# Values in whole rows with edge columns, ones written over them by GpSimd, and a new order table, in a chain of attention, a gated MLP and a gMLP

## The chip, the cores and the metric

The kernel runs on one core of a Trainium2 chip. That core has engines that work side by side, each through its own queue: TensorE (PE: matmuls, and PEld for its weight loads), VectorE (DVE), ScalarE (ACT), GpSimd (POOL) and SyncE (SP), which here issues nearly all DMAs. The metric is the device time of one execution in microseconds (us), as a median of several runs.

## The reference

Three layers run one after the other, on 2 batches of 768 positions. The attention has 8 heads of 64 and sees, for each position, the first 8 positions and the 96 last ones, with a slope per head as bias:

```python
keep = is_global | is_local
dist = np.where(is_global & ~is_local, float(n_local), np.abs(rel).astype(np.float32))
scores = scale * np.matmul(q, k.transpose(0, 1, 3, 2)) + -slopes[:, None, None] * dist
scores = np.where(keep, scores, -1000000000.0)
a = np.exp(scores - np.max(scores, axis=-1, keepdims=True))
a = a / (np.sum(a, axis=-1, keepdims=True) + 1e-09)
x = np.matmul(a, v)
```

Its output, as 768 x 512 per batch, goes into an MLP of width 1024 whose hidden layer is gated by a convolution over positions, and then into a gMLP with a 768 x 768 product over positions:

```python
h = np.maximum(x @ w_in, 0.0)                       # 512 -> 1024
gate = 1.0 / (1.0 + np.exp(-conv_out))              # conv_out: 3 taps over positions of h
x = h * gate @ w_out                                # 1024 -> 512
h = np.maximum(x @ w_in, 0.0)                       # gMLP, 512 -> 1024
u, v = h[..., :512], h[..., 512:]
v_s = np.einsum('ts,bsd->btd', w_spatial, normalized(v)) + b_spatial[None, :, None]
out = (u * v_s) @ w_out                             # 512 -> 512
```

All is fp32. The matmuls of the two MLPs use fp16 pairs, a high half and a low half of each operand (names that end in h and l).

## The kernel before

**Tiling.** A group g is one batch and one of three chunks of 256 positions, so there are six groups. Each group has four head pairs; a pair with its group is a unit u. For a unit the kernel computes score products (line 789, fp32, from a tile `qk`), a reduction with bias and mask and the row's minimum (DVE, line 808), the exponential (ACT, line 826), a transposition of the result on PE (line 839) and the product with the values (line 894), which is divided by its row sum (lines 906 to 911) and transposed again (line 942) into one 128x256 piece of x. PE's high copy of x is written by ACT (456) or DVE (460), the low one by DVE (line 470). Four pieces make the x of a group. Then come eight matmul tasks `inner` of the first MLP (line 1017, twelve matmuls each), which need all four pieces, their convolution and gate, and the outer matmuls (line 1087). The gMLP follows (lines 1171, 1294, 1382, 1444). Weights arrive as packed 128x512 `raw` tiles, are decoded on POOL (659), ACT (655) and DVE (665, 670) and split into high and low halves.

**The values.** Groups 0 and 1 (`PLAINS`) use their values in fp32; the other four split them into halves. The product at line 894 takes 65 columns a head: 64 values and a column of ones, which gives the row sum. The pair's tile therefore has 130 columns (`VW`): a one, 64 values, 64 values, a one. There is a single tile `v_dt_float_89` for both groups. `v_load` (line 726) writes the ones once, by a POOL memset ahead of group 0's load, and loads 128 values at a time between the edge columns, 512 B for each of 12 or 16 pieces of a partition. Group 1's load writes the same inner columns again and leaves the ones.

**The order.** Each piece of work is a task with a list of the tasks it depends on. A table, `ORDER`, lists all tasks: two signs for the task's number, one for its engine (P, D, A, G for POOL, S for SP), and for a task that opens a PSUM bank the number of that bank. `Plan.emit` issues the tasks in that order, so the table fixes the sequence in every engine's queue, including the choice of engine where two could do it; semaphores then only make an instruction wait, they don't change the sequence. `emit` also puts fill-in matmuls on constant data (line 988, 128x256) in front of those PE tasks that the planner expects to wait in the first 70 planned us, in a number that it works out from the planned gap; they are in the program for good.

**DMAs.** SP issues its loads in table order at line 514; a load whose tile is still in use makes SP wait, with all later loads behind it.

## Time and profile before

| | |
|---|---|
| time, median of 3 runs | 346.76 us (346.62 to 347.51) |
| the profiled execution's own time | 346.18 us |
| its span, first to last instruction | 344.4 us |
| mean granted TensorE clock | 0.996 |
| PE busy | 336.9 us (98%) |
| DVE busy | 305.3 us (89%) |
| ACT busy | 244.0 us (71%) |
| POOL busy | 140.6 us (41%) |

The span is cut into stretches in the rows below: how long each engine was busy in a stretch, then the granted clock (1.00 is 2.4 GHz), the mean busy share of the 16 DMA engines and the rate at which they moved bytes. A timeline's row is one run of like instructions with its start and its duration; the bracket, where there is one, gives the idle time just before it and what ended it. Matmuls overlap in PE's pipeline, so the distance between two starts is the time that a matmul costs, and its own duration is longer.

### The profile page before, as it was taken

What the parts mean: (1) busy time and instruction counts of PE and PEld (TensorE: products, weight loads), DVE (VectorE), ACT (ScalarE), POOL (GpSimd) and SP (SyncE); (2) the same over time, 40 slices, a digit from 0 to 9 for tenths busy, and PEclk for the clock granted to TensorE, in tenths of its full rate; (3) what the DMA queues carried; (4) which work ended last, traced back from release to release, by engine and by line L of the source; (5) the groups of instructions that cost most, each with busy time, mean ns of one, the idle gap of its engine ahead of it and who ended that gap; (6) DMA issues with size and microseconds to landing.
All of it is one profiled execution on the core that took longest, in us unless ns stands there. A gap on an engine that the chain in (4) does not pass through costs nothing.

```text
span 344.4 us, 7937 instructions
## 1 busy us (share of the span) xinstructions
PE 336.9 (98%) x2824; PEld 246.5 (72%) x2824; DVE 305.3 (89%) x892; ACT 244.0 (71%) x619; POOL 140.6 (41%) x233
## 2 busy tenths in 40 slices
PE   8999999999999999999999999999999999999993
PEld 5888779898888888888996757755556666654451
DVE  6999999999999999999988899999998999999400
ACT  4999999999999999999865552776555233334331
POOL 5747698599757877737451000000124012010000
PEclk9999999999999999999999999999999999999998
DMA  7999638799659984645770000001461000000332
GB/s 246 349 386 300 214 105 302 175 209 256 125 149 205 278 173 79 184 79 109 102 221 0 2 1 0 2 1 48 126 206 52 0 2 0 3 30 0 124 124 101
DMA packets 46115, 43.62 MB, mean 127 GB/s; under 512 B 34674, under 2 KB 36466, under 8 KB 45554
## 3 DMA queue, kind: packets, MB, share of 16 engines
q1 hardware_dynamic: 46064, 43.02, 45.7%
q8 instruction: 24, 0.39, 0.5%
q14 instruction: 25, 0.20, 0.2%
q10 hardware_dynamic: 2, 0.00, 0.0%
HBM read 31.48 MB, written 3.15 MB: 101 GB/s over the span
## 4 chain that ended last, share of the span: by engine, by line
PE 96%; DMA 1%; DVE 0%; ACT 0%; issue 0%; DVEq 0%
PE bank L1017 19%; PE bank L1087 18%; PE bank L1294 12%; PE bank L1444 9%; PE bank L1382 9%; PE bank L1171 9%; PE bank L789 7%; PE bank L894 4%; PE bank L839 2%; PE bank L988 2%; PE bank L942 2%; DMA qk_dt_float<-in_qk 1%; PE bank L900 1%; PE bank L901 1%; PE bank L902 1%; ACT wk_dt_float L454 0%
## 5 line engine op out<-in xcount | busy, mean ns | idle before, releaser
L1017 PE MATMUL bank<-x_dt_float,w1h_dt_float 128*128 128x260 f16 (+1 forms) x384 | 65.5, 273 | 0.0
L1087 PE MATMUL bank<-hh_dt_float,w2h_dt_float 128*128 128x256 f16 (+2 forms) x192 | 52.4, 273 | 0.0
L1017 PE MATMUL bank<-x_dt_float,w1l_dt_float 128*128 128x260 f16 (+1 forms) x192 | 52.4, 273 | 0.0
L1087 PE MATMUL bank<-hl_dt_float,w2h_dt_float 128*128 128x256 f16 (+2 forms) x192 | 52.3, 272 | 0.0
L1087 PE MATMUL bank<-hh_dt_float,w2l_dt_float 128*128 128x256 f16 (+2 forms) x192 | 52.3, 272 | 0.0
L1030 DVE SCALAR_TENSOR_TENSOR bank<-hp_dt_float,cwt,bank 128x254 f32<-128x254 f32 (+2 forms) x96 | 46.1, 486 | 3.3 <-ACT bank L1024 0.6
L470 POOL TENSOR_TENSOR ph_dt_float<-sb_dt_float,ph_dt_float 128x512 f16<-128x512 f32 x29 | 34.2, 1184 | 20.5 <-ACT ph_dt_float L456 12.4
L1017 PEld LDWEIGHTS <-w1h_dt_float 128*128 128x128 f16 x384 | 37.1, 97 | 5.7
L1087 PEld LDWEIGHTS <-w2h_dt_float 128*128 128x128 f16 x384 | 36.3, 98 | 5.4 <-issue 0.3
L808 DVE CUSTOM_DVE_ANT_0 sb_dt_float<-bank,bias_dt_float 128x256 f32<-128x256 f32 (+1 forms) x96 | 35.4, 402 | 1.6 <-PE bank L789 1.3
L1382 PE MATMUL bank<-ys_dt_float,w3uh_dt_float 128*128 128x384 f16 x128 | 31.2, 326 | 0.0
L826 ACT ACTIVATE sb_dt_float<-sb_dt_float,nb_dt_float 128x256 f32<-128x256 f32 (+1 forms) x64 | 29.6, 491 | 0.0
L659 POOL TENSOR_SCALAR raw_dt_float<-raw_dt_float 128x512 int32<-128x512 uint8 x28 | 19.0, 680 | 24.7 <-DMA raw_dt_float<-in_w 22.0
L1444 PE MATMUL bank<-w4h_dt_float,g_dt_float 128*128 128x512 f16 (+1 forms) x104 | 28.8, 363 | 0.0
L1171 PE MATMUL bank<-w3vh_dt_float,ys_dt_float 128*128 128x512 f16 x96 | 28.5, 379 | 0.0
L470 POOL TENSOR_TENSOR hl_dt_float<-ac_dt_float,hh_dt_float 128x254 f16<-128x254 f32 (+2 forms) x35 | 23.4, 678 | 10.7 <-DVE hh_dt_float L460 8.0
L1444 PEld LDWEIGHTS <-g_dt_float 128*128 128x128 f16 x156 | 15.2, 98 | 15.4
L1171 PEld LDWEIGHTS <-ys_dt_float 128*128 128x128 f16 x144 | 14.1, 98 | 15.3
L1294 PE MATMUL bank<-ws_dt_float,vn_dt_float 128*128 128x384 f16 x144 | 25.0, 326 | 0.0
L1050 ACT ACTIVATE bank<-bank 128x254 f32<-128x254 f32 (+2 forms) x48 | 16.9, 364 | 10.5 <-DVE bank L1030 10.2
L1024 ACT ACTIVATE bank<-hp_dt_float,cwt 128x254 f32<-128x254 f32 (+2 forms) x44 | 21.0, 477 | 0.5
L1055 DVE SCALAR_TENSOR_TENSOR ac_dt_float<-bank,hp_dt_float 128x254 f32<-128x254 f32 (+2 forms) x48 | 19.5, 418 | 2.0 <-ACT bank L1050 1.5
(198 smaller groups left out, 907.6 us busy)
## 6 DMA issues: line engine op xcount, KB each, us to landing
raw_dt_float<-in_w SPq DMA_DIRECT2D x20, 512.0 KB, 6.3
qk_dt_float<-in_qk SPq DMA_DIRECT2D x24, 336.0 KB, 4.6
v_dt_float<-in_vb SPq DMA_DIRECT2D x4, 1024.0 KB, 5.7
out_x<-wk_dt_float SPq DMA_DIRECT2D x11, 256.0 KB, 2.0
raw_dt_float<-in_wst SPq DMA_DIRECT2D x6, 384.0 KB, 3.8
raw_dt_float<-in_w3v SPq DMA_DIRECT2D x4, 512.0 KB, 5.5
raw_dt_float<-in_w3u SPq DMA_DIRECT2D x4, 512.0 KB, 4.4
v_dt_float<-in_vb SPq DMA_DIRECT2D x2, 768.0 KB, 5.1
```

The source lines that it names most:

```text
L470: self.engines[e].tensor_tensor(out=out, in0=in0, in1=in1, op=ALU.subtract)
L789: nc.tensor.matmul(self.ps(sp[h])[:, 256 * t : 256 * (t + 1)], x[r, t * P : (t + 1) * P], y[r, k0[t] : k0[t] + 256], start=n == 0, stop=n ...
L808: nc.vector.tensor_tensor_reduce(out=sb[:, h, :n], in0=self.ps(self.sp[u][h])[:, 256 * t : 256 * t + n], in1=self.m("bias", 2 * p + h)[:, ...
L826: nc.scalar.activation(out=sb[:, h, :n], in_=sb[:, h, :n], func=AF.Exp, scale=-1.0, bias=nb[:, h : h + 1])
L1017: nc.tensor.matmul(self.ps(acc)[:, :nx], w[f][:, k * P : (k + 1) * P], x[:, k, x0:], start=k == n == 0, stop=k == 3 and n == 2,)
L1024: nc.scalar.activation(out=ac(), in_=near(1), func=AF.Copy, scale=tap(1))
L1030: nc.vector.scalar_tensor_tensor(out=ac(), in0=near(j), scalar=tap(j), in1=ac(), op0=ALU.mult, op1=ALU.add)
L1087: nc.tensor.matmul(ps(), w[2 * d + k // 4][:, k % 4 * P : (k % 4 + 1) * P], x, start=k == n == 0, stop=k == 7 and n == 2,)
L1171: nc.tensor.matmul(ps(), x[:, y, k, tk], w[k], start=n == 0, stop=n == 11)
L1294: self.nc.tensor.matmul(self.ps(acc)[:, :HS], v[:, k, x, ek], w[:, k, y], start=n == 0, stop=n == 8)
L1382: nc.tensor.matmul(ps(), w[e4][:, k * P : (k + 1) * P], x[:, y, k, s], start=n == 0, stop=n == 11)
L1444: nc.tensor.matmul(ps(), x[:, y, k, tk], w[k][:, at], start=n == 0, stop=n == 11)
```

## The change

The host now packs a second array of values, `vp`, for groups 0 and 1: the layout of the tile with its edge columns, filled with copies of the neighbouring values. `v_load` loads whole rows of it, 1560 or 2080 floats a partition, 6,240 or 8,320 B in one piece. The load covers the edge columns too, so the memset of the ones is now a task behind each load, two in all. The whole order table is replaced. Lines from 735 of the kernel before on carry numbers that are three lower in the kernel after.

```diff
 ORDER = (
-    "CHSAAGAWSDnGAnSAXGABDACGAZSADDAuSAbGAgSAEDBHGCMDAFPAGDCJA0CIGAHDAaP12AJDAKAASAAIDAMAAoGAdDBaSApA3AyDAYSANGAcDAOA",
...
+    "AAGAWSCISEIGAuSAbGABDBIGDoGAnSADDAZSD2GACGAgSAEDCNDAFPAaP12CKA0AGDCJGFLGAHDAJDAQAASAAIDBiP34BbSAKAA0DAoGAMAAdDAX",
...
 class Kernel:
-    def __init__(self, ctx, tc, vb, qk, qf, kf, vf, nw, w1, cw, w2, w3u, w3v, wst, bsp, w4, out):
+    def __init__(self, ctx, tc, vb, vp, qk, qf, kf, vf, nw, w1, cw, w2, w3u, w3v, wst, bsp, w4, out):
...
         if g in PLAINS:
-            v = self.m("v").rearrange("p (n d) -> p n d", d=VW)
-            if g == 0:
-                self.ones_beside(v, ("v", g, "one"))
-            self.load(
-                v[:, : n * NPAIR, 1 : 1 + 2 * D], self.vb[b, c, :, :n].rearrange("p a (n d) -> p (a n) d", d=2 * D),
-                [("v", g, "v")], n * P * 2048, [("v", g, "one")],
-            )
+            size = n * NPAIR * VW
+            v = self.m("v")[:, :size]
+            self.load(v, self.vp[g, :, :size], [("v", g)], 4 * P * size)
+            self.ones_beside(v.rearrange("p (n d) -> p n d", d=VW), ("v", g, "one"))
             return
...
     vb = np.stack(rows, axis=1).reshape(B, NCH, 4, P, DM).transpose(0, 1, 3, 2, 4)
+    vp = vb.reshape(B * NCH, P, 4, NPAIR, 2 * D)[: len(PLAINS)]
+    vp = np.concatenate([vp[..., :1], vp, vp[..., -1:]], axis=-1).reshape(len(PLAINS), P, -1)
```

The new table moves instructions on every engine. Three places follow; the names are tiles, and the number behind a name is its buffer. First DVE, before the kernel's first matmul of line 1017. `x_dt_float_156` is the low half of x for group 0, and its row is the last of the four pieces. This is the queue of the kernel before:

```order
L911 TENSOR_TENSOR xk_dt_float_159<-bank,r_dt_float_161 128x256
L670 SCALAR_TENSOR_TENSOR wk_dt_float_138<-raw_dt_float_137,bank 128x512
L665 SCALAR_TENSOR_TENSOR bank<-bank,raw_dt_float_126 128x512
L470 TENSOR_TENSOR x_dt_float_156<-bank,x_dt_float_155 128x256
L808 ISA sb_dt_float_132,nm_dt_float_147<-bank,bias_dt_float_82 128x256
L808 ISA nm_dt_float_147 128x1
L670 SCALAR_TENSOR_TENSOR wk_dt_float_136<-raw_dt_float_126,bank 128x512
```

And this is the same place after:

```order
L908 TENSOR_TENSOR xk_dt_float_159<-bank,r_dt_float_161 128x256
L665 SCALAR_TENSOR_TENSOR bank<-bank,raw_dt_float_126 128x512
L805 ISA sb_dt_float_139,nm_dt_float_153<-bank,bias_dt_float_82 128x256
L805 ISA nm_dt_float_153 128x1
L805 ISA sb_dt_float_139,nm_dt_float_153<-bank,bias_dt_float_83 128x256
L805 ISA nm_dt_float_153 128x1
L470 TENSOR_TENSOR x_dt_float_156<-bank,x_dt_float_155 128x256
L670 SCALAR_TENSOR_TENSOR wk_dt_float_136<-raw_dt_float_126,bank 128x512
```

Two reductions of a later unit (line 805, with the short row that reads out their minimum) stand ahead of the piece of x instead of one behind it; a decoding step (line 670) has left the place.

The second place is SP's queue, where the loads of about 33 to 50 us stand; the two `raw` loads of `in_w` are those that the trace shows from 38.60 us on. Before:

```order
L514 DMA qk_dt_float_122<-in_qk 128x672
L514 DMA raw_dt_float_128<-in_w 128x512
L514 DMA raw_dt_float_137<-in_w 128x512
L514 DMA qk_dt_float_88<-in_qk 128x672 x2
L514 DMA qk_dt_float_130<-in_qk 128x672
L514 DMA raw_dt_float_142<-in_w3v 128x512
```

After:

```order
L514 DMA qk_dt_float_122<-in_qk 128x672
L514 DMA raw_dt_float_128<-in_w 128x512
L514 DMA qk_dt_float_88<-in_qk 128x672
L514 DMA qk_dt_float_130<-in_qk 128x672
L514 DMA raw_dt_float_137<-in_w 128x512
L514 DMA qk_dt_float_122<-in_qk 128x672
L514 DMA qk_dt_float_88<-in_qk 128x672
L514 DMA v_dt_float_89<-in_vb 128x2048
```

Two `qk` loads have moved ahead of the second `raw` load.

The third place is POOL's queue around the second memset of the ones, which the kernel before doesn't have; there the single memset stands at the queue's beginning. After:

```order
L659 TENSOR_SCALAR raw_dt_float_126<-raw_dt_float_126 128x512
L1036 MEMSET hp_dt_float_178 128x1
L659 TENSOR_SCALAR raw_dt_float_137<-raw_dt_float_137 128x512
L659 TENSOR_SCALAR raw_dt_float_142<-raw_dt_float_142 128x512
L729 MEMSET v_dt_float_89 128x16x2
L470 TENSOR_TENSOR w1l_dt_float_103<-wk_dt_float_129,w1h_dt_float_95 128x512
```

The memset (line 729) stands behind three decodes of `raw` tiles (line 659). On SP, the loads of two of these three, `raw_dt_float_126` and `raw_dt_float_142`, are issued behind the load of `v`. The first memset of the kernel after stands on POOL behind two decodes and six mask sums (line 607).

## Rows read from the trace of the kernel before

**Rows 1.** The page: busy time, share, instructions; shares of the last chain.

```profile
PE 336.9 (98%) x2824; PEld 246.5 (72%) x2824; DVE 305.3 (89%) x892; ACT 244.0 (71%) x619; POOL 140.6 (41%) x233
...
PE 96%; DMA 1%; DVE 0%; ACT 0%; issue 0%; DVEq 0%
```

**Rows 2.** By stretch: us, busy PE, PEld, DVE, ACT, POOL, clock, DMA, GB/s.

```profile
0.00:70.00 70.00, 68.20 (x550) 55.68 (x551) 64.78 (x222) 64.06 (x157) 47.55 (x85) 1.00 0.77 259
70.00:340.00 270.00, 268.71 (x2277) 190.80 (x2274) 240.51 (x671) 179.97 (x463) 93.03 (x149) 1.00 0.39 93
...
10.00:20.00 10.00, 10.00 (x84) 8.51 (x83) 9.25 (x38) 9.89 (x23) 7.98 (x12) 1.00 1.05 378
20.00:30.00 10.00, 9.88 (x86) 8.50 (x85) 9.24 (x29) 9.58 (x23) 4.99 (x6) 1.00 0.89 315
```

**Rows 3.** Timeline of the end: start, us, engine, line, operation.

```profile
338.33 0.38 PE L1444 MATMUL bank<-w4l_dt_float,g_dt_float 128*128 128x512 f16 x1
```

**Rows 4.** Line 988 alone: count, ns min/median/max, first and last start.

```profile
L988 PE MATMUL bank<-hl_dt_float x60: 272/273/421, 1.2 to 53.0; 128*128 128x256 f16 x60
```

**Rows 5.** Timeline of PE from 39 to 56 us.

```profile
42.00 1.04 PE L988 MATMUL bank<-hl_dt_float 128*128 128x256 f16 x8
...
48.94 0.93 PE L988 MATMUL bank<-hl_dt_float 128*128 128x256 f16 x7
50.10 1.14 PE L789 MATMUL bank<-qk_dt_float 64*128 64x256 f32 x8 [0.23 <-DMA qk_dt_float<-in_qk]
```

**Rows 6.** Timeline of PE around the first matmul of line 1017.

```profile
28.03 0.38 PE L1017 MATMUL bank<-x_dt_float,w1h_dt_float 128*128 128x256 f16 x2
...
29.34 0.38 PE L1017 MATMUL bank<-x_dt_float,w1h_dt_float 128*128 128x256 f16 x2
```

**Rows 7.** Timeline of DVE around the last piece of group 0's x.

```profile
27.06 0.41 DVE L470 TENSOR_TENSOR x_dt_float<-bank,x_dt_float 128x256 f16<-128x256 f32 x1
27.39 0.41 DVE L808 CUSTOM_DVE_ANT_0 sb_dt_float<-bank,bias_dt_float 128x256 f32<-128x256 f32 x1
27.73 0.08 DVE L808 DVE_READ_ACCUMULATOR2_ANT nm_dt_float<- 128x1 f32 x1
```

**Rows 8.** Timeline of SP's queue: start of the issue, us, what is loaded.

```profile
7.98 0.39 SPq L514 DMA_DIRECT2D v_dt_float<-in_vb  x1
...
25.11 0.68 SPq L514 DMA_DIRECT2D v_dt_float<-in_vb  x1
...
28.48 4.52 SPq L514 DMA_DIRECT2D raw_dt_float<-in_w  x4
...
38.60 6.49 SPq L514 DMA_DIRECT2D raw_dt_float<-in_w  x2
```

**Rows 9.** By stretch, as rows 2, where the v loads and others move.

```profile
10.00:12.50 2.50, 2.50 (x22) 1.87 (x22) 2.23 (x11) 2.49 (x7) 2.26 (x4) 1.00 1.06 301
...
21.00:24.00 3.00, 2.88 (x27) 2.59 (x26) 2.67 (x13) 2.83 (x7) 0.02 (x1) 1.00 1.03 412
27.00:30.00 3.00, 3.00 (x29) 2.58 (x28) 2.79 (x8) 2.93 (x7) 2.13 (x3) 1.00 0.88 272
```

**Rows 10.** Timeline of PE at the first product with v.

```profile
13.22 0.66 PE L839 MATMUL bank<-ident,sb_dt_float 128*128 128x128 f32 x4
13.71 0.56 PE L894 MATMUL bank<-v_dt_float,pt_dt_float 128*128 128x65 f32 x4
```

**Rows 11.** Timeline of POOL, at its start and before 14 us.

```profile
1.40 0.14 POOL L732 MEMSET v_dt_float<- 128x32 f32 x1
...
12.87 0.99 POOL L607 TENSOR_TENSOR bias_dt_float<-bias_dt_float,keep_dt_float 128x288 f32<-128x288 f32 x1 [0.45 <-DVE nm_dt_float L808]
```

**Rows 12.** The page: POOL's decodes; raw loads, last number median us to landing.

```profile
L659 POOL TENSOR_SCALAR raw_dt_float<-raw_dt_float 128x512 int32<-128x512 uint8 x28 | 19.0, 680 | 24.7 <-DMA raw_dt_float<-in_w 22.0
...
raw_dt_float<-in_w SPq DMA_DIRECT2D x20, 512.0 KB, 6.3
```

**Rows 13.** Waits before 60 us: us in total, times, longest.

```profile
POOL raw_dt_float L659 <- DMA raw_dt_float<-in_w: 9.3, 3, 4.5
```

More of the change, by code (lines that the diff above doesn't have):

```diff
@@ L170 @@
+    "DcoDcLDcpP4cnDcXDcYGcxP1crDcRGctDcvDb4GdiP5dQDdRDc0P0dSDb-Db_DcAAauDdrP7cEDa7DcGAcFDa8DcqDc9Dc3DdDP4c4Dc-DdoP2dE",
+    "DcdDc_DceGdADdBDdJP6dpAcyDdsAdqScMAdtSdcP2dKDcSAdWDcZAdjDduP7cfAczDc1DdXDdkDdlDd3P1dFDddDdTDdGDdeDdfDdxP0c5Dd4Ad",
+    "HDd5Sc6GdLDdgDdmDd0P5dMDdyAdvDclAdNDdwSc7AdYDdzSdCAdZDdaDd_P4dIAdOAdUAdbAeLP2dhAeADdnAd1AeCP1d2SeBSd6P6d8P7d7DeM",
+    "AeDAeNSeOP0d9Ad-SeESeIP3eFP4ePAeJAeQSeKSeGAeHS",
 )
@@ L1692, in pack @@
     arrays = dict(
-        vb=vb, qk=qk, qf=qt, kf=kt, vf=vfull,
+        vb=vb, vp=vp, qk=qk, qf=qt, kf=kt, vf=vfull,
         nw=np.stack([np.asarray(n_global), np.asarray(n_local)]).astype(np.int64).view(np.uint16),
```

106 lines of the change are left out of this document (51 added, 55 removed).

## The prediction

> **What bounds the kernel now.** I read the page from the top and then went to the trace. TensorE (PE) is busy 336.9 us of the 344.4 us span, and the chain that ended last is 96% PE [rows 1]. A busy PE need not be a useful one, so the next view is the one by stretch [rows 2]: from 70 to 340 us PE is busy 268.71 us, and its last matmul begins at 338.33 [rows 3], so next to nothing is idle in between. The first 70 us are different. There PE lacks 1.80 us, and part of what counts as busy is no work at all: 60 fill-in matmuls on constant data (line 988), all between 1.2 and 53.0 us [rows 4]. In the same stretch, from 10 us on, DVE and ACT are busy 9.2 to 10 us of every 10 [rows 2]. So the kernel has two parts: an opening in which DVE and ACT feed PE and the gaps are filled with line 988, and 270 us in which PE alone sets the pace. What the opening loses is not given back, because PE has no gap later in which to catch up. The change can therefore move the end by what it does to PE in the opening, and by what it does to the last few us.
>
> **The fill-in matmuls.** They stand in PE's queue and run whether needed or not, so their number is a cost of the program itself. Eight of them take 1.04 us [rows 5], of which the last one's own 0.27 [rows 4]: (1.04 - 0.27) / 7 = 0.11 us each. Counted in the two orders, the program before has 60 and the program after 66. Fifteen stand before the first score products in both. Before the first matmul of line 1017 there are 30 before and 38 after: +8 x 0.11 = +0.88. Behind it, 30 before and 28 after: -2 x 0.11 = -0.22. Together +0.66 us.
>
> **The DVE piece behind those eight.** The first matmul of line 1017 (28.03) [rows 6] needs the last of four 128x256 pieces of x, which DVE began to write at 27.06 [rows 7]. In the new order four more line-808 reductions of 256 columns stand ahead of that piece (two of them are in the fences on DVE). One takes 27.39 to 27.73, 0.34 us, to the next instruction's start [rows 7], so 4 x 0.34 = 1.36 us more DVE work. DVE has little room there, 9.24 us of the 10 from 20 to 30 us are busy [rows 2], so little of the 1.36 can be hidden. The eight fills already occupy 0.88 of it. What is left is between 0 (hidden) and 0.48 us; I take 0.25, the middle.
>
> **The queue of SP at 45 us.** PE ran seven fills from 48.94 and started the score products only at 50.10, named as released by the DMA of a qk load [rows 5]: 1.16 us, of which 7 x 0.11 = 0.77 were fills and 0.39 bare waiting. That load stood behind two raw loads that waited for their buffers, 6.49 us from 38.60 [rows 8]; the new order puts it and the next qk load ahead of the second of them (the fences on SP). The fills are counted already. The bare 0.39 us may go, between 0 and 0.39; I take 0.2 as gained.
>
> **The loads themselves.** The first v load is issued at 7.98 [rows 8] and its 512-byte pieces (12 for each of 128 partitions) flow at 301 GB/s in the stretch behind, with the DMA engines at 1.06, where raw and qk loads reach 412 GB/s at 1.03 [rows 9]. Moved at 412, its 128 x 6,240 B = 0.80 MB take 1.94 us in place of 0.79 MB / 301 = 2.61 us: 0.7 us of DMA time saved. For the second, 1.05 MB at the 272 GB/s of its stretch [rows 9] is 3.86 us, and 1.065 MB at 412 would be 2.58: 1.3 saved. None of it lies on the path: PE entered the first product with v at 13.71 with no idle named there, straight behind a transposition at 13.22 [rows 10]. What the freed DMA time gives to the raw and qk loads behind it is the rival below. If the loads stay slow, this term stays nil as well.
>
> The Trainium skill, "DMA: Bandwidth & Descriptors", section "Specifications", puts the least transfer for line rate at 512 B, and these pieces are exactly 512 B. By that the whole-row form saves nothing, the loads keep their length and only the memset's lateness would grow. The trace disagrees, 301 against 412 GB/s, so the measurement decides.
>
> **The memsets of the ones.** One memset before (0.14 us at 1.40) [rows 11], two after. They stand on POOL, which is busy 140.6 of 344.4 us [rows 1], so their own time costs at most 0.3 us there and nothing on PE. The new thing is the wait: POOL now waits for the v load to land, with its decodes and low halves of the weights queued behind it, and PE's v products wait for POOL. The first has two decodes and six mask sums (line 607) ahead of it in the new order; before, POOL began the last of these sums at 12.87 and it took 0.99 [rows 11], so POOL comes to the memset near 12 to 14 us, about when the load is in; bounds 0 to 0.5 us. I take 0, since four more fills (0.44 us) stand on PE ahead of the first product with v, 27 against 23. The second memset is a rival.
>
> **The end.** The last two PE tasks, their ACT copies and the last output load are the same in both orders. From the start of the last matmul (338.33) [rows 3] to the end of the span at 344.4 nothing changes: 0, within +-0.2.
>
> **Sum.** +0.66 + 0.25 - 0.2 + 0 = +0.7 us (between +0.3 and +1.2). The profiled execution took 346.18 us, 0.58 below the median of the three runs, 346.76. Profiled, the new kernel would take 346.9; against the median 347.5.
>
> **Rivals.**
> *The second memset is late (slower).* In the new POOL order the memset over group 1's v stands behind three raw decodes, two of whose loads are issued behind that v load. Before, PE's product with it needed the load alone. PE gets to it in the new order at about 28.03 + 0.88 (first line-1017 product), five products of 1.31 (28.03 to 29.34) [rows 6], one score product of 1.14 [rows 5], two transpositions of 0.49 (13.22 to 13.71) [rows 10] and a fill: 37.7 us. The v load of before went out at 25.11 and the raw loads behind it from 28.48 over 4.52 us, so the last near 32.6 [rows 8]; a raw load lands in 6.3 us (median), 38.9, one decode is 0.68 (19.0 us / 28) [rows 12], memset by 39.6: 1.9 us late. With the v load 1.3 us shorter the price is 0.6. It decides from the point where that memset ends after 37.7. For it: POOL waited 9.3 us for raw loads in the first 60 us, the longest 4.5 [rows 13]. Against: the raw load that went out at 28.48 need not be as late if buffers free sooner. Time: 347.5 + 0.6 to 1.9, so about 349.
>
> *The gaps close (faster).* The bare waits of PE around the fills shrink: 0.39 at 50.10 [rows 5], and a part of the 1.80 us that PE lacks in the first 70 [rows 2], most of it in the first 10. An estimate from the two for what can close is 1.1 us, while the fills stay at +0.66: -0.4 us, 346.3. And where DMA is full, above 1.0 from 10 to 20 us [rows 2], the 0.7 us saved on the first v load may bring everything behind it forward by as much, decodes and x pieces included: -1.1, 345.7. Against it: DVE has more to do before the first line-1017 product, and the fills are there to be run in any case.
>
> *The change does not do what it says.* The rows are split again by the DMA engines, 272 GB/s stays: only the memset rival grows, to 349.4.
>
> **How the numbers follow.** A measurement of this kernel can tell about 0.3% (1.04 us) from no change. Forecast case (+0.3 to +1.2, a seventh of it beyond 1.04): 0.58. Late memset or another new wait in the opening (+1.0 to +2.9): 0.24. Closing gaps (-1.6 to +0.2): 0.18, six tenths of it beyond 0.3%. So faster 0.11, slower 0.08 + 0.23 = 0.31, within 0.58. The range takes in the forecast with both bounds, the closing gaps down to -1.1 and the late memset to its upper part: 345.7 to 349.1.
>
> **What the new profile would show.** The first matmul of line 1014 (1017 before) at 28.9 to 29.4. Line 985 (988 before) 66 times. The score product that started at 50.10 no longer ends a wait for DMA. A stretch from 70 us on with PE idle nowhere. More than 400 GB/s while the first v load moves, and no PE wait named after POOL's memset of v. I am wrong if the first product of group 1 waits for that memset, if PE shows idle time after 70 us, or if the opening ends no later than before although it holds six more fills.

## The result, and the profile after

The kernel after takes 349.44 us (median of 10 runs, 348.11 to 352.22), the kernel before took 347.08 in the same session (10 runs, 346.39 to 347.51). The ratio is 1.0075, with an interval of [1.0047, 1.0102]: slower, by 2.4 us where +0.7 was forecast, and above the range's end of 349.1. The profiled execution took 348.64 us, its span is 346.6, its mean granted clock 0.999.

The page of after, against [rows 1] (busy time, share, instructions; shares of the last chain):

```profile
PE 337.3 (97%) x2830; PEld 246.9 (71%) x2830; DVE 302.4 (87%) x874; ACT 244.9 (71%) x625; POOL 155.1 (45%) x246
...
PE 82%; DVE 6%; DMA 5%; issue 2%; POOL 2%; ACT 1%; SPq 0%; DVEq 0%; ACTq 0%; POOLq 0%
```

PE works only 0.4 us more. The chain that ended last was 96% PE before; now 14% of it runs through DVE, DMA, POOL and ACT: PE is waiting for others in places where it didn't. By stretch, with the columns of [rows 2]:

```profile
0.00:70.00 70.00, 66.69 (x545) 54.91 (x546) 64.69 (x222) 63.08 (x153) 47.43 (x85) 1.00 0.76 250
70.00:340.00 270.00, 269.50 (x2284) 191.68 (x2282) 237.75 (x655) 181.26 (x472) 107.66 (x162) 1.00 0.38 95
```

In the first 70 us PE lacks 3.31 us where it lacked 1.80: 1.51 more, and 6 fills (0.66) come on top. Behind it 0.50 us are idle. The tail is as long as before; its start is 2.36 us later than in [rows 3]:

```profile
340.69 0.38 PE L1441 MATMUL bank<-w4l_dt_float,g_dt_float 128*128 128x512 f16 x1
```

The view of waits says which of PE's waits are named in the first 100 us (total, times, longest). Of after:

```profile
PE bank L985 <- DVE hl_dt_float L538: 1.2, 1, 1.2
PE bank L891 <- POOL v_dt_float L729: 1.0, 2, 0.5
PE bank L786 <- DMA qk_dt_float<-in_qk: 0.9, 2, 0.7
PE bank L1014 <- DVE xk_dt_float L908: 0.3, 1, 0.3
```

The first row is the start of the program and stands in before too. The other three are new or grown: before, PE never waited for the memset or for line 908's tile, and only 0.23 us for a qk load [rows 5]. In PE's timeline (start, us, operation, and in the bracket the idle time just ahead of it and its releaser) the five waits are these:

```profile
8.54 1.13 PE L786 MATMUL bank<-qk_dt_float 64*128 64x256 f32 x8 [0.69 <-DMA qk_dt_float<-in_qk]
...
14.02 2.00 PE L891 MATMUL bank<-v_dt_float,pt_dt_float 128*128 128x65 f32 x16 [0.47 <-POOL v_dt_float L729]
...
37.98 2.00 PE L891 MATMUL bank<-v_dt_float,pt_dt_float 128*128 128x65 f32 x16 [0.51 <-POOL v_dt_float L729]
...
40.17 1.13 PE L786 MATMUL bank<-qk_dt_float 64*128 64x256 f32 x8 [0.20 <-DMA qk_dt_float<-in_qk]
...
80.44 0.38 PE L1014 MATMUL bank<-x_dt_float,w1h_dt_float 128*128 128x260 f16 x2 [0.34 <-DVE xk_dt_float L908]
```

They add up to 2.21 us, close to the 2.36 by which the end moved. That such a list is not yet a cause is what the experiments had to show: taking away two of these waits changed nothing.

### The profile page after: what moved, and what is told of

Read it like the earlier page. It is cut to its first block, busy times and chain, and to the rows that moved or that the text cites. A ratio compares the mean times of both kernels' runs of the same rounds, so it can differ in the third digit from the quotient of the medians.

```text
span 346.6 us, 7949 instructions
## 1 busy us (share of the span) xinstructions
PE 337.3 (97%) x2830; PEld 246.9 (71%) x2830; DVE 302.4 (87%) x874; ACT 244.9 (71%) x625; POOL 155.1 (45%) x246
## 2 busy tenths in 40 slices
DMA packets 44707, 43.65 MB, mean 126 GB/s; under 512 B 34674, under 2 KB 34930, under 8 KB 44146
## 4 chain that ended last, share of the span: by engine, by line
PE 82%; DVE 6%; DMA 5%; issue 2%; POOL 2%; ACT 1%; SPq 0%; DVEq 0%; ACTq 0%; POOLq 0%
PE bank L1084 17%; PE bank L1014 14%; PE bank L1291 12%; PE bank L1441 9%; PE bank L1379 9%; PE bank L1168 9%; PE bank L786 4%; DMA pt_dt_float<-ph_dt_float 2%; PE bank L891 2%; DMA qk_dt_float<-in_qk 2%; DVE bank L665 2%; PE bank L939 2%; POOL bias_dt_float L607 1%; PE bank L897 1%; PE bank L899 1%
## 5 line engine op out<-in xcount | busy, mean ns | idle before, releaser
L1084 PE MATMUL bank<-hh_dt_float,w2h_dt_float 128*128 128x254 f16 (+2 forms) x192 | 52.3, 273 | 0.1
L1084 PE MATMUL bank<-hh_dt_float,w2l_dt_float 128*128 128x254 f16 (+2 forms) x192 | 52.3, 273 | 0.0
L1084 PE MATMUL bank<-hl_dt_float,w2h_dt_float 128*128 128x254 f16 (+2 forms) x192 | 52.3, 273 | 0.0
L470 POOL TENSOR_TENSOR hl_dt_float<-ac_dt_float,hh_dt_float 128x254 f16<-128x254 f32 (+2 forms) x37 | 25.0, 684 | 16.9 <-ACT hh_dt_float L456 13.2
L1441 PEld LDWEIGHTS <-g_dt_float 128*128 128x128 f16 x156 | 15.2, 98 | 15.4
L1358 ACT ACTIVATE hp_dt_float<-bank 128x260 f32<-128x260 f32 (+1 forms) x44 | 16.7, 382 | 6.6 <-DVE ac_dt_float L1052 3.3
L454 ACT ACTIVATE wk_dt_float<-bank 128x512 f32<-128x512 f32 (+1 forms) x11 | 5.8, 555 | 21.6 <-PE bank L1441 15.6
```

The source lines that it names most:

```text
L470: self.engines[e].tensor_tensor(out=out, in0=in0, in1=in1, op=ALU.subtract)
L1084: nc.tensor.matmul(ps(), w[2 * d + k // 4][:, k % 4 * P : (k % 4 + 1) * P], x, start=k == n == 0, stop=k == 7 and n == 2,)
L1441: nc.tensor.matmul(ps(), x[:, y, k, tk], w[k][:, at], start=n == 0, stop=n == 11)
```

## Experiments: the loads, the memsets and the table apart

In all of these, the fills stand in fixed places and number (those of the table that the kernel uses), so that an edit doesn't move them.

**e1_load_only.** The new loads and both memsets under the old table; the second memset's task was put on POOL behind the low half of w2's first block (at 33.70 us in its trace). The head of the loop over a load's pieces and the old memset, which go as well, are left out of the cut ("...").

```diff
...
-            self.load(
-                v[:, : n * NPAIR, 1 : 1 + 2 * D], self.vb[b, c, :, :n].rearrange("p a (n d) -> p (a n) d", d=2 * D),
+            self.load(v, self.vp[g, :, :size], [("v", g)], 4 * P * size)
+            self.ones_beside(v.rearrange("p (n d) -> p n d", d=VW), ("v", g, "one"))
```

> The new load alone: the kernel before, with its own order and its 60 fill-in matmuls at their places, but values of groups 0 and 1 in whole rows and two memsets of the ones behind them. The first memset stands on POOL where the changed kernel has it, behind the six mask sums; the second stands right behind the low half of w2's first block, near 32.5 us. Theory TABLE (the new order is what costs, the load is nothing): within 0.5 us of before, 346.6 to 347.6. Theory MEMSET (PE's products with v wait for memsets that POOL reaches late, 0.7 us at the first and 0.6 at the second in the changed kernel): about +0.3 us, since here only the first can be late (13.9 against a product that started at 13.71), 347.4. Theory ROWS (whole rows move no faster or slower and hold up the loads behind them, as the second v load took 7.2 us to land against 6.5 before): +0.7 to +1.5 us, 347.8 to 348.6.

Measured: 347.07 us, ratio 0.9994 [0.9983, 1.0005]. The new form of the loads and the memsets are free under the old order; they save nothing either. By the pages, the packets between 512 B and 2 KB went from 36,466 less 34,674 = 1,792 before to 34,931 less 34,675 = 256 in e1. The 1,536 that went are the 12 x 128 pieces of the first load alone. The second load already moved in long packets before: from 25 to 31 us that trace has none between 512 B and 2 KB and 129 of 8 KB or more. And the DMA engines moved more at a smaller share: where [rows 9] has 301 GB/s at a busy share of 1.06 from 10 to 12.5 us, e1 has

```profile
10.00:12.50 2.50, 2.50 (x21) 1.60 (x18) 1.55 (x9) 1.48 (x5) 2.19 (x4) 1.00 1.01 406
```

(the last two numbers). The stretch holds other loads too. PE is full in it in both, and the time is the same: nothing waits for what was saved.

**e2_table_only.** The new table and its 66 fills on the old loads, with a single memset at the start.

```diff
...
+            if g == 0:
+                self.ones_beside(v, ("v", g, "one"))
+            self.load(
+                v[:, : n * NPAIR, 1 : 1 + 2 * D], self.vb[b, c, :, :n].rearrange("p a (n d) -> p (a n) d", d=2 * D),
-            self.load(v, self.vp[g, :, :size], [("v", g)], 4 * P * size)
-            self.ones_beside(v.rearrange("p (n d) -> p n d", d=VW), ("v", g, "one"))
```

> The new order alone: the changed kernel's order and its 66 fill-in matmuls, but the old loads of 512-byte pieces and one memset of the ones at POOL's start. Theory TABLE: like the changed kernel, 349 to 349.5. Theory MEMSET: the changed kernel less what PE waits there for the two memsets, 0.5 to 1.2 us, so 348.2 to 348.9. Theory ROWS: 0.7 or more below the changed kernel, with the loads behind the second v load landing 0.7 earlier than there.

Measured: 350.58 us, 1.0099 [1.0063, 1.0136]. The whole loss is the table's, with the old loads too.

**e3_ones_loaded.** The kernel after without its memsets: here the host writes the ones into the edge columns of `vp`, so the two POOL instructions are left out.

```diff
-            self.ones_beside(v.rearrange("p (n d) -> p n d", d=VW), ("v", g, "one"))
...
-    vp = np.concatenate([vp[..., :1], vp, vp[..., -1:]], axis=-1).reshape(len(PLAINS), P, -1)
+    one = np.ones_like(vp[..., :1])
+    vp = np.concatenate([one, vp, one], axis=-1).reshape(len(PLAINS), P, -1)
```

> The changed kernel with its order and fills, but the edge columns in memory hold ones already, so both memsets are left out; whole rows are loaded as there. Theory TABLE: 349 to 349.5, no gain above 0.3 us. Theory MEMSET: 0.5 to 1.2 us less than the changed kernel, 348.2 to 348.9, and PE's first product with v begins right behind the transposition ahead of it. Theory ROWS: as the changed kernel, 349.4.

Measured: 349.41 us, 1.0069 [1.0038, 1.0101], the time of after. Both named waits for POOL are gone, and nothing is won. The profiled run took 350.98 us, 1.6 above the median. PE's timeline in it shows the next releaser at once: the product with v runs without a wait, and PE stands longer at the next score products, which it reaches at about 40.1 us as in after:

```profile
38.19 1.90 PE L890 MATMUL bank<-v_dt_float,pt_dt_float 128*128 128x65 f32 x16
...
41.30 2.08 PE L785 MATMUL bank<-qk_dt_float 64*128 64x256 f32 x8 [1.21 <-DVE r_dt_float L902]
```

The bracket names DVE, the event that came last by the record; the qk load of this unit (unit 7, `qk_dt_float_122`) landed at 41.16 and is what PE needed (in after it landed at 40.03). In e2, which has no late memset either, the same wait is 1.71 us and the record names the load itself. The windows of e3 show the clock behind such a stand (columns as in [rows 2]; the clock is the third number from the end):

```profile
40.00:42.00 2.00, 0.79 (x5) 0.68 (x6) 1.84 (x6) 1.94 (x5) 1.91 (x3) 0.82 0.87 286
42.00:44.00 2.00, 2.00 (x12) 1.29 (x9) 0.59 (x3) 0.00 (x0) 1.86 (x6) 0.50 0.40 153
44.00:46.00 2.00, 2.00 (x17) 1.83 (x16) 1.16 (x7) 1.41 (x3) 0.00 (x0) 0.83 0.00 0
```

After PE stood still its granted clock was 0.50, the level of 1.2 GHz, through 42 to 44 us. An estimate from these two rows: beside the 1.21 us of the wait, 2 us at half the clock lose another 1.0. A stand does not always bring this. In e2 the longer one, 1.71 us at the same place, left the clock at 1.00:

```profile
41.77 1.14 PE L789 MATMUL bank<-qk_dt_float 64*128 64x256 f32 x8 [1.71 <-DMA qk_dt_float<-in_qk]
...
42.00:44.00 2.00, 2.00 (x19) 1.65 (x18) 1.06 (x5) 0.41 (x1) 1.79 (x6) 1.00 0.31 121
```

What decides between the two is not shown.

## Experiments: which stretch of the table

**e4_new_then_old** and **e5_old_then_new** join the two tables at the 440th task, near 65 us (written here as lists of tasks; tasks that would stand twice or not at all are kept once). Behind the joint the PSUM banks were given out anew. The loads are the new ones in both.

```diff
-ORDER = after[:440] + after[440:]
+ORDER = after[:440] + before[440:]   (e4)
+ORDER = before[:440] + after[440:]   (e5)
```

> The changed kernel with its order up to its 440th task (PE at about 65 us), and the order of the kernel before for all tasks that are left, with the PSUM banks given out anew from there. The traces of the two kernels put PE 1.2 us behind by 65 us and another 1.0 us behind between 70 and 80 us. If both are made by the order of their own stretch: 348.3 (+1.2 on before). If the second is only the first one's consequence (the same transfers, later): 349.4 as the changed kernel. If the opening costs nothing lasting and the later order makes all of it: 347.1.

> New loads and memsets, the order of the kernel before up to its 440th task (PE at about 65 us), and the new order for all tasks left. Theory OPENING-AND-LATER (the new order costs in both halves, about 1.2 and 1.0 us): 1.0 us above before, 348.2. Theory OPENING (all of the loss is the opening's, and what shows between 70 and 85 us is its consequence): as before, within 0.4 us.

Measured: e4 348.74 us, 1.0053 [1.0033, 1.0073]; e5 348.41 us against 346.94, 1.0044 [1.0026, 1.0061]. So the loss has two parts, each of about 1.5 to 1.8 us, and together they are rather more than the whole. That the part behind 65 us costs anything was in none of the prediction's cases.

A sum along PE's timeline shows where after falls behind: each matmul's distance to the next start, less the median distance of matmuls of the same line, shape and tiles in the two traces, with fills counted in full. Waits, slow clock and fills all go into it. By 40 us the sum is 9.4 us in before and 10.8 in after; by 70, 14.9 and 16.1; by 90, 15.4 and 17.6; by 200, 16.9 and 19.2. About half of the 2.3 us comes before 70 us, half between 70 and 90, and nothing later. From 75 to 80 us alone it is 0.1 in before and 1.2 in after. The busy time by stretch, on which the prediction rested, doesn't show the second half, since matmuls that run slowly or wait inside a row count as busy. In e5 the later loss sits elsewhere in part: a wait of 0.63 us at 71.58, and more between 80 and 90.

## Experiments: the opening

**e6_qk7_early.** After, with two moves: unit 7's qk load ahead of three raw loads on SP, and the second memset ahead of three decodes on POOL.

```diff
+L514 DMA qk_dt_float_122<-in_qk 128x672
 L514 DMA raw_dt_float_142<-in_w 128x512
 L514 DMA raw_dt_float_135<-in_w 128x512
 L514 DMA raw_dt_float_143<-in_w 128x512
-L514 DMA qk_dt_float_122<-in_qk 128x672
...
+L729 MEMSET v_dt_float_89 128x16x2
 L659 TENSOR_SCALAR raw_dt_float_126<-raw_dt_float_126 128x512
 L1036 MEMSET hp_dt_float_178 128x1
 L659 TENSOR_SCALAR raw_dt_float_137<-raw_dt_float_137 128x512
 L659 TENSOR_SCALAR raw_dt_float_142<-raw_dt_float_142 128x512
-L729 MEMSET v_dt_float_89 128x16x2
```

> The changed kernel with two tasks moved: the load of qk for unit 7 goes from behind three raw loads to ahead of them on SP, and the second memset of the ones to ahead of the decode that stands before it. The trace of the kernel with ones in memory shows PE idle for 1.2 us at 40 us in front of that unit's score products, waiting for that load, and the granted clock at 0.50 from 42 to 44 us behind it. Theory QK7 (this wait, and the clock that falls behind it in some executions, is the larger part of the loss and of the spread): 0.7 to 1.5 us below the changed kernel, 347.9 to 348.7, and no execution above 350.5. Theory FILLS (the fills at places where their successor is ready are the loss): no change beyond 0.3 us in the median.

Measured: 348.52 us (347.89 to 349.07), 1.0042 [1.0027, 1.0058]; some 0.9 us less than after by the medians (the two intervals overlap), and no run above 349.1 where after reached 352.2. Both waits are gone, and no third takes their place there:

```profile
37.58 1.90 PE L891 MATMUL bank<-v_dt_float,pt_dt_float 128*128 128x65 f32 x16
...
39.40 1.14 PE L786 MATMUL bank<-qk_dt_float 64*128 64x256 f32 x8
```

Before, this load landed at 39.42 and PE wanted it at 40.10: 0.7 us of slack. In after it landed at 40.03 and PE was there already.

**e13_qk7_alone.** The first of the two moves without the second.

```diff
+L514 DMA qk_dt_float_122<-in_qk 128x672
 L514 DMA raw_dt_float_142<-in_w 128x512
 L514 DMA raw_dt_float_135<-in_w 128x512
 L514 DMA raw_dt_float_143<-in_w 128x512
-L514 DMA qk_dt_float_122<-in_qk 128x672
```

> The changed kernel with unit 7's qk load ahead of the three raw loads, and the second memset of the ones left at its place behind the decodes. With both moved it took 348.52. Theory QK7 (the load alone is the cause): the same, 348.3 to 348.8. Theory MEMSET (with the load in time, the memset is what PE waits for, later than before since the raw load ahead of its decodes lands 0.8 us later): 0.4 to 1.0 us above that, 348.9 to 349.5, and a PE wait of 1 us or more in front of the first product with group 1's v, named after the memset.

Measured: 349.45 us, 1.0083 [1.0054, 1.0112], no better than after. With the load out of the way the memset is the wait:

```profile
38.88 1.33 PE L891 MATMUL bank<-v_dt_float,pt_dt_float 128*128 128x65 f32 x10 [0.73 <-POOL v_dt_float L729]
```

So the memset and the load stand one behind the other: taking away the memset (e3) leaves the load, taking away the load (e13) leaves the memset, and only both together pay, here 0.9 us and in e9, below, 1.6.

**e9_qk7_then_old.** The tasks of e6 up to the 440th, then the order of before.

```diff
-ORDER = e6[:440] + after[440:]
+ORDER = e6[:440] + before[440:]
```

> The changed kernel with unit 7's qk load and the second memset moved ahead, as in the experiment before, up to the 440th task, and the order of the kernel before for the rest. Theory TWO HALVES (the opening's loss sits at 40 us and the later loss between 70 and 90 us, where PSUM banks come back late from DVE, and they add): 1.0 us below the kernel with the moved load alone, 347.5, so about 0.4 to 0.6 us above before. Theory ONE CHAIN (an earlier PE only waits for the same late transfers and banks): no change beyond 0.3 us, 348.5.

Measured: 347.57 us against 347.13, 1.0008 [0.9992, 1.0024]. Compared with e4, which has the same later half, the two moves take away nearly all of the opening's loss: 0.0053 - 0.0008 = 0.0045, 1.6 us, with intervals that don't meet. What e6 still loses lies behind 65 us.

**e7_few_fills.** After without 24 of its 66 fills: those of 10, 4, 3, 6 and 1 between 48 and 61 us, in front of tasks whose inputs the trace showed as long ready.

```diff
-FILLS = {..., 304: 2, 398: 10, 350: 4, 383: 3, 448: 6, 436: 1}
+FILLS = {..., 304: 2}
```

> The changed kernel without 24 of its 66 fill-in matmuls: the 10, 4, 3, 6 and 1 that stand between 48 and 61 us in front of tasks whose inputs had been ready for 5 us or more in its trace. Theory FILLS (a fill in front of a ready task is pure cost, 0.11 us each): 2.6 us less than the changed kernel, 346.8. Theory NEXT (PE only comes earlier to what is late anyway, the transposed load that it waited for at 76.8 us): less than 1 us gained, 348.5 or more, with the wait at that place about 2 us long.

Measured: 349.89 us, 1.0088 [1.0073, 1.0104]: if anything slower than after, although 24 x 0.11 = 2.6 us of work was taken out. In after the ten fills stand so:

```profile
48.70 1.25 PE L985 MATMUL bank<-hl_dt_float 128*128 128x256 f16 x10
50.03 2.00 PE L891 MATMUL bank<-v_dt_float,pt_dt_float 128*128 128x65 f32 x16
```

and in e7, without them, the same product starts no earlier, and the clock behind it falls:

```profile
50.68 2.81 PE L891 MATMUL bank<-v_dt_float,pt_dt_float 128*128 128x65 f32 x16 [1.17 <-DVE nm_dt_float L805]
...
50.00:52.00 2.00, 1.32 (x10) 1.32 (x11) 1.97 (x8) 2.00 (x4) 1.67 (x4) 0.92 0.19 74
52.00:54.00 2.00, 2.00 (x11) 2.00 (x12) 2.00 (x5) 1.23 (x4) 1.75 (x5) 0.50 0.00 0
```

Its inputs were ready; what it lacked was a PSUM bank, which DVE gives back when its reduction (line 805) has read it. The fills covered that wait, and in after the clock is 1.00 from 50 to 54 us. Five of e7's six runs have a mean clock of 0.995 or less.

**e10_qk9_early.** Before, with the qk load that PE waited for at 50.10 [rows 5] ahead of a raw load, and without the seven fills there (so 53 fills).

```diff
+L514 DMA qk_dt_float_88<-in_qk 128x672
 L514 DMA raw_dt_float_137<-in_w 128x512
-L514 DMA qk_dt_float_88<-in_qk 128x672
```

> The kernel before, with its own loads and order, but the load of qk for unit 9 ahead of the raw load that waits for its buffer (the new order's idea at 45 us, by itself), and without the 7 fill-in matmuls in front of that unit's score products, 53 in all. Theory QUEUE (PE waits 1.2 us there for that load, as at 50.10 in the trace): 0.4 to 1.2 us below before, 345.8 to 346.6. Theory NEXT (DVE's and ACT's pace sets the opening, and PE meets the next late bank a few us on): within 0.3 us of before.

Measured: 347.10 us, 1.0006 [0.9988, 1.0025]. No gain. PE stands at the same place for DVE instead (line 1055):

```profile
49.79 1.45 PE L789 MATMUL bank<-qk_dt_float 64*128 64x256 f32 x8 [0.38 <-DVE ac_dt_float L1055]
```

**e11_new_start.** e10, with its first 44 tasks in the new order, whose first loads are arranged otherwise.

```diff
-ORDER = e10[:44] + e10[44:]
+ORDER = after[:44] + e10[44:]
```

> As the experiment with unit 9's load moved in the kernel before, and also the new order's first 44 tasks (to about 9 us: another order of the first five loads and of the first score products). In the traces PE has 0.5 to 1.5 us less behind it at 10 us with the new order's start and has lost that again by 20 us, waiting for a load, an exponential and v. Theory START (that loss comes from the new order's tasks between 10 and 20 us): 0.5 us or more below the experiment without the new start. Theory LOADS (the new start makes PE wait for the first loads later, whatever follows): no gain, up to 0.5 us slower.

Measured: 347.48 us, 1.0015 [0.9997, 1.0032]. The wait of 0.69 us at 8.54 in after has little or no effect on the end.

## Experiments: from 65 to 90 us

**e8_later_scores.** After, with a matmul task of line 1014 (`I6` in the table) moved ahead of the score products (`JV`) and the transposition (`Hu`) of later units on PE, in other banks; nine tasks behind them change banks to fit. Theory: PE's wait at 80.44 is one for a bank.

```diff
-JVP15 ... HuP6 I0D I6P0
+I6P1 JVP56 ... HuP0 I0D
```

> The changed kernel with one PE task moved: the first of two inner tasks near 80 us goes ahead of the score products that stand before it, so that it opens a PSUM bank that was free at 78.2 us and not the one that DVE gives back at 80.4. Theory BANKS (the new order holds all eight banks there, and PE waits for DVE to give one back): 0.6 to 0.9 us below the changed kernel, 348.5 to 348.8, and no PE wait named after line 908 at 80 us. Theory LATE (the transposed load is late, and the wait moves to the next task): no change beyond 0.3 us.

Measured: 350.65 us, 1.0117 [1.0089, 1.0145], no faster than after and, if anything, slower (the intervals overlap). The wait moved to the next such task and grew, and its releaser is another line:

```profile
83.12 0.38 PE L1014 MATMUL bank<-x_dt_float,w1h_dt_float 128*128 128x260 f16 x2 [0.95 <-DVE x_dt_float L470]
```

**e12_one_bank.** e5, with the wait that its trace shows at 71.58 (0.63 us, named after DVE's line 466) taken away by another bank for that task of line 1014 (7 for 2). Five tasks behind it exchange 2 and 7 as well, and no task changes place. In the table:

```diff
-IBP2 ... InP7 ... IbP32 ... JZP2 ... JWP7 ... JhP7
+IBP7 ... InP2 ... IbP37 ... JZP7 ... JWP2 ... JhP2
```

> The kernel with the old order up to 65 us and the new one behind it, with PSUM banks alone changed: the inner task near 71.6 us, which waited 0.63 us for DVE to give bank 2 back while bank 7 had not been used since 60 us, opens bank 7, and the tasks behind it take the banks that this leaves free. No instruction moves. Theory BANKS (the later half of the new order costs by banks that come back late): 0.4 to 0.7 us below the kernel with the old order first, 347.7 to 348.0, and no PE wait at 71.6. Theory PACE (DVE's and the transposed loads' pace between 70 and 90 us sets it; banks only show where PE meets it): no change beyond 0.3 us, the same sum of waits by 90 us, at other tasks.

Measured: 349.11 us against 346.96, 1.0052 [1.0034, 1.0070], no better than e5. PE ran on and stood later, for the data of a transposed load:

```profile
77.52 0.20 PE L897 MATMUL bank<-vh_dt_float,pt_dt_float 128*128 128x65 f16 x1 [0.15 <-DMA pt_dt_float<-ph_dt_float]
```

These two give the bank theory no support: when PE was let through, it stood later for something else that was late. The windows from 75 to 80 us, of before first and then of after, show which engines (behind PE and PEld: busy DVE and ACT):

```profile
75.00:80.00 5.00, 5.00 (x68) 4.40 (x66) 4.89 (x18) 4.99 (x12) 4.10 (x6) 1.00 1.05 172
```

```profile
75.00:80.00 5.00, 4.83 (x66) 3.94 (x64) 3.40 (x10) 3.35 (x10) 1.93 (x3) 1.00 0.75 151
```

ACT and DVE were full before and each idle for about 1.6 us after. ACT's timeline in after has the reason:

```profile
74.54 0.63 ACT L454 ACTIVATE vh_dt_float<-v_dt_float 128x512 f16<-128x512 f32 x1
76.81 0.62 ACT L456 CAST ph_dt_float<-sb_dt_float 128x512 f16<-128x512 f32 x1 [1.65 <-DMA pt_dt_float<-ph_dt_float]
77.34 0.65 ACT L454 ACTIVATE ys_dt_float<-bank 128x254 f16<-128x254 f32 x2
```

The copy at 76.81 writes `ph_dt_float_206`, which an earlier transposed load still reads. ACT stands for it, and behind it are two copies of `ys` whose banks have been full for a while. DVE needs them, and its timeline has a hole of its own:

```profile
77.75 0.42 DVE L466 SCALAR_TENSOR_TENSOR ys_dt_float<-bank,ys_dt_float 128x254 f16<-128x254 f32 x1 [1.37 <-ACT ys_dt_float L454]
```

A little later PE's score products stop in the middle of a row, without a bracket: one step of two matmuls takes 0.72 us where those before it take 0.28. In e6, which the next two runs start from, it is this one:

```profile
78.06 0.72 PE L786 MATMUL bank<-qh_dt_float32r 64*128 64x256 f32 x2
...
78.39 0.18 PEld L786 LDWEIGHTS bank<-qh_dt_float32r 64*128 64x128 f32 x1 [0.27 <-DVE ac_dt_float L1052]
```

The weight load behind the stop waits for DVE. PE also waits for that transposed load itself, a wait that the five above leave out since it stands in the queue of weight loads. In after:

```profile
76.78 0.10 PEld L897 LDWEIGHTS <-pt_dt_float 128*128 128x128 f16 x1 [0.38 <-DMA pt_dt_float<-ph_dt_float]
```

Whether line 908's xk, for which PE waits at 80.44, is late because of ACT's copy was open. Two runs tested the chain at either end.

**e14_v3_later.** e6, with the 0.79 MB load of group 3's values behind the transposed load that ACT waited for.

```diff
+L862 DMA_TRANSPOSE pt_dt_float_144<-ph_dt_float_206 128x16x128
 L514 DMA v_dt_float_89<-in_vb 128x1536
-L862 DMA_TRANSPOSE pt_dt_float_144<-ph_dt_float_206 128x16x128
```

> The kernel with unit 7's qk load and the second memset moved (348.52), and one thing more: the 1 MB load of group 3's v goes from just ahead of the transposed load of unit 9 on SP to just behind it. In the traces with the new order that transposed load lands 7.9 to 8.6 us after its issue and PE waits for it at 77 us; with the old order behind 65 us it lands in 6.3 to 6.7 us. Theory TRANSPOSED (the v load ahead holds it up, and all that PE waits for between 76 and 82 us follows from it: the product, its division on DVE, the bank): it lands in 4.5 to 6 us, the waits at 77 to 82 us go, 0.7 to 1.1 us less, 347.4 to 347.8. Theory PACE (DVE gives banks back late in the new order whatever lands when): no change beyond 0.3 us, 348.2 to 348.8.

Measured: 348.50 us against 347.17, 1.0038 [1.0021, 1.0055], like e6. The transposed load now landed 4.39 us after its issue, at 72.48, and neither ACT nor PE waited for it any more; but ACT waited for the values instead:

```profile
75.20 0.63 ACT L454 ACTIVATE vh_dt_float<-v_dt_float 128x512 f16<-128x512 f32 x1 [1.98 <-DMA v_dt_float<-in_vb]
```

**e15_ph_behind.** e6, with ACT's copy to `ph_dt_float_206` behind the two copies of `ys` and a step of the gate (line 1047), which were ready.

```diff
+L454 ACTIVATE ys_0_dt_float_205<-bank 128x254 x2
+L1047 ACTIVATE bank<-bank 128x256
 L456 CAST ph_dt_float_206<-sb_dt_float_139 128x512
-L454 ACTIVATE ys_0_dt_float_205<-bank 128x254 x2
-L1047 ACTIVATE bank<-bank 128x256
```

> The kernel with unit 7's qk load and the second memset moved (348.52), and one ACT task moved: the copy of ph for unit 11, which in the new order waits 1.6 us at 75 us for the transposed load of unit 9 to have read the buffer it writes, goes behind the two copies of ys and the gate step that stood behind it and had been ready. Theory ACT QUEUE (ACT waits in order for that load, DVE behind ACT, PE behind DVE's banks): 0.6 to 1.0 us less, 347.5 to 347.9, DVE and ACT busy over 4 us of the 5 from 75 to 80 us, and no PE wait at 80 us. Theory PACE (something else is late in the new order): no change beyond 0.3 us, 348.2 to 348.8.

Measured: 348.03 us against 347.12, 1.0020 [1.0006, 1.0034], where e6 has 1.0042 and e14 1.0038, each against before in its own session: 0.8 and 0.6 us less, though the intervals overlap a little. ACT uses the time of the load's flight, and the wait shrinks from 1.65 us in after to 0.69:

```profile
74.70 0.68 ACT L454 ACTIVATE ys_dt_float<-bank 128x254 f16<-128x254 f32 x2
75.37 0.37 ACT L1047 ACTIVATE bank<-bank 128x256 f32<-128x256 f32 x1
76.42 0.62 ACT L456 CAST ph_dt_float<-sb_dt_float 128x512 f16<-128x512 f32 x1 [0.69 <-DMA pt_dt_float<-ph_dt_float]
...
75.00:80.00 5.00, 4.54 (x66) 3.73 (x65) 4.34 (x14) 4.32 (x12) 2.82 (x3) 1.00 0.74 139
```

The last row is the window of e15. This is the same window of e6:

```profile
75.00:80.00 5.00, 4.55 (x62) 3.58 (x60) 3.50 (x10) 3.56 (x9) 2.00 (x3) 1.00 0.74 143
```

DVE and ACT are busy 0.84 and 0.76 us more in e15 than in e6, by one instruction's place on ACT, with the same loads and the same PE order. The stop inside the score products is gone:

```profile
78.04 0.28 PE L786 MATMUL bank<-qh_dt_float32r 64*128 64x256 f32 x2
...
79.64 0.38 PE L1014 MATMUL bank<-x_dt_float,w1h_dt_float 128*128 128x260 f16 x2 [0.36 <-DVE xk_dt_float L908]
```

The second row is the miss: the wait for xk, 0.32 us in e6, stays. So the chain from ACT over DVE to the score products is shown; that xk is late by it is not.

**e16_qk1_early.** e15, with unit 1's qk load ahead of the first raw load, and the first memset ahead of the last mask sum: the waits at 8.54 and 14.02.

```diff
+L514 DMA qk_dt_float_122<-in_qk 128x672
 L514 DMA raw_dt_float_128<-in_w 128x512
-L514 DMA qk_dt_float_122<-in_qk 128x672
...
+L729 MEMSET v_dt_float_89 128x12x2
 L607 TENSOR_TENSOR bias_dt_float_86<-bias_dt_float_86,keep_dt_float_80 128x288
-L729 MEMSET v_dt_float_89 128x12x2
```

> The same, and two tasks moved at the start: unit 1's qk load ahead of the first raw load, and the first memset of the ones ahead of the last mask sum on POOL. In the traces with the new order PE waits 0.8 to 1 us at 9 us for that qk load, 0.3 to 0.5 us at 12 us for an exponential behind it, and 0.4 to 0.8 us at 14 us for v or its memset. Theory START (this late load shifts all that follows, since PE later only runs at full pace): 0.5 to 1.2 us below the kernel without these two moves, 346.5 to 347.3. Theory GIVEN BACK (the raw load lands later instead, and DVE and ACT pass that on): no change beyond 0.3 us.

Measured: 348.17 us, 1.0027 [1.0013, 1.0040], no better than e15. As in e11, what PE loses in the first 14 us is not what the end is late by.

**What stays open.** e15 is still 0.7 us above before by its ratio, 0.2 to 1.2 by the interval. The opening that it shares with e9 accounts for 0.3 us of that [-0.3, 0.8]; the remainder, about 0.4 us, lies behind 65 us by the same comparison. Its trace still shows PE standing there for the transposed load (0.38 us at 76.39) and for xk (0.36 at 79.64); whether either is the remainder was not tried. No version ran faster than before.

## Why the prediction was wrong, point by point

**The opening alone.** The step that failed first was in the part on what bounds the kernel: PE has no idle time from 70 us on [rows 2], "so next to nothing is idle in between", and only the opening and the last few us can move the end. That nothing is idle there is true of the old order and says nothing of the new one, which re-sorts the queues of ACT and DVE up to 90 us and beyond. In [rows 2] ACT and DVE are busy 9.2 to 10 of every 10 us in the opening; the window 75 to 80 shows them as full (4.89 and 4.99 of 5) there too. I hadn't looked at how full they are behind 70, and so held PE's lack of waits for slack: the later stretch was put at nothing. By e5 this missing term is +1.5 us [0.9, 2.1]. The text's own sign, that it is wrong "if PE shows idle time after 70 us", was met as well, by 0.50 us. The opening, for its part, was put at +0.7 by fills and a DVE piece, and lost 1.8 by e4: by e3, e13, e6 and e9 most of that is the second memset and unit 7's qk load, one behind the other. The prediction had the first as a rival and the second not at all.

**The fills, +0.66.** The count was right: 66, and the rows show them.

```profile
L985 PE MATMUL bank<-hl_dt_float x66: 272/273/421, 1.2 to 59.7; 128*128 128x256 f16 x66
```

The price was not: a fill costs 0.11 only where PE would otherwise have run on. Where PE would have stood, it is free, and by e7 taking out 24 wins nothing. The six more seem to cost little: e9 has all 66 and is 0.3 us above before [-0.3, 0.8]. No run isolates them.

**The DVE piece, +0.25.** About right. The first matmul of line 1014 was forecast at 28.9 to 29.4 and came at 28.61, behind its fills and the end of DVE's piece:

```profile
27.27 1.25 PE L985 MATMUL bank<-hl_dt_float 128*128 128x256 f16 x10
28.61 0.38 PE L1014 MATMUL bank<-x_dt_float,w1h_dt_float 128*128 128x256 f16 x2
...
28.13 0.42 DVE L470 TENSOR_TENSOR x_dt_float<-bank,x_dt_float 128x256 f16<-128x256 f32 x1
```

Ten fills at 0.11 us are through at about 28.37, and the piece ends at 28.55, so some 0.24 us beyond the fills went to DVE. The whole came out only 0.58 later than before (28.03), where 0.88 + 0.25 were expected. PE was ahead from the start: by the sum of start-to-start distances it had lost 5.4 us by 10 us, against 6.2 in before.

**SP's queue, -0.2.** The score products at 50.10 indeed no longer end a wait for DMA, as the text said. But e10 shows that this wins nothing: another wait, for a bank, ends 0.3 us earlier. And it was the wrong end of the queue. At unit 7 the new order took the 0.7 us of slack that a load had, with no wait in the old trace to warn of it; waits of 1.21 us (e3) and 1.71 (e2) came of that where the memset didn't come first.

**The loads, 0.** Right (e1), and for the reason given: none of it lies on the path. The rate rose above the 400 GB/s of the forecast under the old order (406 in e1 from 10 to 12.5 us), but not in after, where the same stretch has 324 at 0.94. The rival "gaps close", which wanted the saved DMA time to bring everything forward, was not borne out: e1's interval ends at -0.17%. For the second load the 1.3 us had no base. It already moved in long packets before (e1 above), so the 272 GB/s of its stretch has another reason, which is not shown. The Trainium skill ("DMA: Bandwidth & Descriptors", section "Specifications") holds 512 B for enough for line rate. The rates of this case differ from that: 301 GB/s at a share of 1.06 with pieces of 512 B became 406 at 1.01 in e1 with rows of 6,240 B under the same order. The time can't decide it, since the load is off the path.

**The memsets.** The first was taken as nil; PE waited 0.47 us for it, and e16 shows that this didn't matter. The second was the rival "late memset", forecast at 0.6 to 1.9 us late at 37.7; PE came to it at about 37.5 and waited 0.51. Half right: the place and the mechanism were there, and its sentence "I am wrong if the first product of group 1 waits for that memset" was met. But as the cause it was incomplete. Removing it alone won nothing (e3); with the qk load it was worth 0.9 us in e6 (by medians that overlap), or 1.6 by e4 against e9. The rival was costed as if nothing else were late behind it.

**The end, 0.** Right: from the start of the last matmul to the end of the span it is 346.6 - 340.69 = 5.91 us after and 344.4 - 338.33 = 6.07 before.

**The sum and the range.** +0.7 was forecast and +2.4 measured. The range's upper end, 349.1, took in most of the late memset's 0.6 to 1.9; it left out that an opening that loses 1.8 us (e4) and a later stretch that loses 1.5 (e5) can come together.

## What to carry to other kernels

A searched order that is replaced as a whole has to be costed as a whole: for each engine that feeds the bottleneck, ask in every stretch how full it is and which loads land just ahead of their use, not only where the old trace shows a wait. A named wait is worth what the next one behind it leaves, so test waits in pairs before you call one the cause. And in an in-order queue, look for an instruction that must wait for a reader of its output buffer (here a transposed load) and stands ahead of ready work: moving it behind that work costs nothing and was worth about 0.7 us here, by intervals that overlap a little.

## What the runs showed that I had not expected

- After PE stood still for 1.2 us, its granted clock was at 0.50 (1.2 GHz) for some 2 us at two different places: 42 to 44 us in e3, and 52 to 54 in e7. Such a stand cost about twice what its bracket says, by the estimate from e3. But behind one of 1.71 us (e2, at 40 us) the clock stayed at 1.00, so the length alone does not decide.
- The fills are worth more than their 0.11 us: without 24 of them the kernel was not faster (1.0088 [1.0073, 1.0104], after 1.0075).
- The form of a load can change the DMA's own rate (301 to 406 GB/s in e1) and its packets (1,792 to 256 of a class) and leave the time where it was. And of two loads written alike, in pieces of 512 B, one moved in such packets and the other in none so short.
- After, its runs spread over 4.1 us (348.1 to 352.2), before over 1.1. In e6 (6 runs) the spread is 1.2 again, while e13, with the memset still late, reaches 352.2 too. That points to the waits near 38 to 41 us. In after the time goes with the mean granted clock of the run: five runs at 0.998 or 0.999 took 348.1 to 349.5 us (median 348.6), five at 0.993 to 0.995 took 349.4 to 352.2, and e6 has no run under 0.995. So part of what e6 wins over after, perhaps most, is the runs in which the clock fell. e4 and e9 differ by more than that: e4's five runs at 0.996 or more took 348.1 to 348.8, and e9's median is 347.6.
